# First token block of the experts stage taken through seven block products, with its first weight set prepared inside the attention

## The chip, the cores and the metric

One core of a Trainium2 chip runs the whole program. The metric is the device time of one execution in microseconds (us); the median of three runs is given, and one further execution was recorded by the hardware profiler. TensorE is PE in the rows (its weight loads PEld), VectorE DVE, ScalarE ACT, GpSimd POOL, and SP is the engine that issues DMAs.

## The reference

An attention with a bias that a small network makes from relative positions is followed by a dense layer that takes the maximum of three products:

```python
scores = scale * np.matmul(q, k.transpose(0, 1, 3, 2)) + bias   # (4, 8, 576, 576)
attn = exp(scores - max); attn /= sum(attn) + 1e-9
attn_out = np.matmul(attn, v)                                   # (4, 8, 576, 64)
x = attn_out.transpose(0, 2, 1, 3).reshape(2304, 512)
h = np.maximum(np.maximum(x @ w1, x @ w2), x @ w3)              # 2304 x 768
out = h @ w_out                                                 # 2304 x 512
```

## The kernel before, in words

**Stages.** A bias stage (0 to about 47 us of the trace) makes the bias; the attention follows (to 262 us), then the products with w1, w2, w3 (to 463 us, `moe`) and the products with w_out (to the end). Every product of the last two stages is made of three matmuls on values split into a high and a low half (`high` is a cast on ScalarE, `low` a subtraction on VectorE or GpSimd): high by high, low by high, high by low.

**The attention** runs in 72 steps (`Attention.step`, step n = 9 * pair + y, where y = 4 is a mixed step of leftovers), and four more that drain it (72 to 75). Step n makes the scores of step n (`front`, tile `s`), turns the exponentials of step n-4 on TensorE (`flip`, tiles `tp` and `lp`, one buffer each way, freed by copies `et` on ScalarE and VectorE), multiplies turned blocks by v (`pv`), then adds bias and takes the maximum on VectorE (`shift`, `sn`, `nm`), takes the exponentials on ScalarE (`expo`, tile `e`) and normalizes those of step n-2 on GpSimd (`norm`, with the reciprocal `rc` on VectorE in even steps). The order of each engine is the order of the program text; no engine overtakes itself.

**Work placed into the steps.** `step(n, more)` calls the entries of `more` at two places: `between()` stands behind the step's exponentials (in steps 18 to 71 ahead of `norm`, in the drain behind it) and moves each entry by one piece of vector or GpSimd work; at the step's end one entry moves by one piece of ScalarE work. The entries are generators that mark which kind comes next: `w0` (`first`, conversion of three weight sets of 64-bit values to 32 bits, five pieces for each half of a set), `pend` (queued pieces on GpSimd, in steps with y = 3, 5, 8), `ex` (`early_x`) and `lx` (`late_x`), which split the first token block into halves. `prep` puts casts and low halves of q and k into the steps with y = 0, 1, 3, 4.

**Token blocks and weight sets.** The attention's output lies in blocks b11, b12, b21, b22 of three token blocks x = 0, 1, 2 (`raws`, slots `r{x}_{k}`, k = 0 to 3 for b12, b11, b21, b22). A weight set s is a 512 x 256 part of one of w1, w2, w3; there are nine. Sets 1 to 8 use seven block products (`group`), for which each token block also needs the sums t1 = b12 - b11, t3 = b22 - b12, t2 = t3 + b11, t4 = b21 - t2 and each set four sums of its blocks. Set 0 is multiplied with all three token blocks in eight block products each (`plain`). One block product is six matmuls of 384 columns (`terms`). A product may add onto the PSUM bank of an earlier one (`made(p, on)`); before that the earlier value has been copied out.

**Slots.** A tile takes the slot of its tag. Where an older tile of the same tag is still in use, the first writer of the new tile waits for every reader of the old one, also for readers that stand behind it in the program text. `home` (class `Blocks`) puts the high half of t3 into r{x}_0, its low half into r{x}_1, and those of t2 into r{x}_2 and r{x}_3, the slots of raw b12, b11, b21 and b22.

**Order of the products before.** plain(0), plain(1), plain(2), then the groups of set 1. `jobs` holds, for each product slot, the casts, sums and low halves of token blocks that are emitted ahead of it.

Of the kernel before, what the change touches and what calls it, by code (L numbers as in the profile page):

```python
# [19 lines left out]
def kernel(  # L20
# [191 lines left out]
    class Attention:  # L212
# [204 lines left out]
        def step(self, n, more=()):  # L417
# [36 lines left out]
            def empty():  # L454
                tp0, tp1, left = self.flip(f)
                if lead and n < NSTEP:
                    for h in range(2):
                        self.shift(n, h)
                    if split:
                        self.expo(n, 0)  # L460
                shared = n < NS + 2
                for x in tp0 + ([] if shared else left):
                    nc.scalar.copy(*x)  # L463
                if turned:
                    products()
                for x in tp1 + (left if shared else []):
                    nc.vector.tensor_copy(*x)  # L467
# [172 lines left out]
    def moe(pool, wpool, x0, xa, xb, raw, sr):  # L640
# [15 lines left out]
        def plain(x, slot):  # L656
            for t in range(2):
                for b in range(2):
                    o = bank(f"c{b}{t}_{x}")[:, 0:TW]
                    for d in range(2):  # L660
                        n = (("b11", "b12"), ("b21", "b22"))[d][t]
                        terms(o, wf[0], xs[x][n], 256 * (2 * d + b), d == 0, d == 1)
                        if d:
                            nc.scalar.copy(ht[:, x, 2 * b + t], o)
                        slot()

        def group(s, x):
# [14 lines left out]
            def p1():  # L682
                o["m1"] = keep("m1", 2)
                nc.scalar.copy(o["m1"], made("p1"))
# [50 lines left out]
        def raise_w(s, k):  # L735
            raw, sr = made_w[s]
            if k == 0:
                p = wpool if s % 2 == 0 else pool
                wf[s] = tuple(p.tile([128, 1792], F32R, tag=f"w{c}{s % 2}", bufs=1, name=f"w{c}{s}") for c in "hl")
# [12 lines left out]
        for k, what in enumerate((  # L752
                (F(b1.high, "b11", "b21"), F(b0.sum, "t4")),
                (F(b1.low, "b11"), F(b1.high, "b12"), F(b0.high, "t2")),
                (F(b1.low, "b21"), F(b1.high, "b22")),
                (F(b1.low, "b12"),),
                (F(b1.low, "b22"), F(b2.high, "b11")),
                (F(b0.low, "t2"), F(b2.high, "b21")),
                (F(b1.sum, "t1"), F(b2.high, "b12")),
                (F(b2.low, "b11"), F(b2.high, "b22"), F(b1.high, "t1")),  # L760
                (F(b2.low, "b21"), F(b0.high, "t4")),
                (F(b2.low, "b12"),),
                (F(b2.low, "b22"),),
                (F(b0.low, "t4"),),
                (F(b1.low, "t1"),),
                (F(b1.sum, "t3"),),
                (F(b1.sum, "t2"), F(b1.high, "t3")),
                (F(b1.low, "t3"),),
                (F(b1.sum, "t4"), F(b1.high, "t2")),
                (F(b1.low, "t2"), F(b1.high, "t4")),  # L770
                (F(b1.low, "t4"), F(raise_w, 1, 0)),
                (F(b2.sum, "t1"), F(raise_w, 1, 1)),
                (F(lower_w, 1, 0, v, 3), F(b2.high, "t1")),
                (F(lower_w, 1, 3, v, 4),),
                (F(b2.low, "t1"),),
                (F(b2.sum, "t3"),),
        )):
            at(k // 8, k % 8, *what)
        at(3, 0, F(b2.sum, "t2"), F(b2.high, "t3"))
        at(3, 1, F(b2.low, "t3"))  # L780
        at(3, 3, F(b2.sum, "t4"))
        at(3, 4, F(b2.high, "t2"))
        at(3, 5, F(b2.low, "t2"))
        at(3, 6, F(b2.high, "t4"))
        at(4, 2, F(b2.low, "t4"))
# [228 lines left out]
        def out_pair(m):  # L1014
# [23 lines left out]
            def p1():  # L1038
                o["m1"] = keep("m1", 2)
# [47 lines left out]
        for x in range(NX):  # L1087
            now[:] = [x, 0]
            plain(x, slot)
# [14 lines left out]
    with tc.manual_schedule():  # L1104
# [44 lines left out]
        class Pieces:  # L1149
# [18 lines left out]
        def first():  # L1168
            todo = [(w_srcs(s, d), f"{s}_{d}") for s in (PARK, 0, 1) for d in range(2)]
# [8 lines left out]
            def sums(raw, name, k=None):  # L1178
# [12 lines left out]
                return [lambda n=n: piece(n) for n in range(4)]  # L1191

            def block(name):
                made = []

                def half(d):
                    if d == 0 and name == "2":
                        made.append(apool.tile([128, 1024], F32, name="wr2", bufs=1))
                    elif d == 0:
                        if name == "1":  # L1200
                            pend.rest()
                        made.append(raw_tile(wpool, 1))
                    return made[0][:, 512 * d:512 * d + 512].bitcast(U32)

                return made, half
# [3 lines left out]
            made, half = block("2")  # L1209
            for d in range(2):  # L1210
                yield from conv(lambda: half(d), f"2_{d}")
            nc.sync.dma_start(out=w_d[0, 0], in_=made[0])
            pend.extend(sums(made[0], "2", 0))
            hi, lo = (wpool.tile([128, 1792], F32R, tag=f"w{c}0", bufs=1, name=f"w{c}0") for c in "hl")
            wf[0] = (hi, lo)
            made, half = block("0")
            for d in range(2):
                r = slice(512 * d, 512 * d + 512)
                yield from conv(lambda: half(d), f"0_{d}")
                raw = made[0]  # L1220
                yield "scalar"
                nc.scalar.copy(hi[:, r], raw[:, r])
                pend.extend(lambda k=k, raw=raw: arith(nc.gpsimd, part(lo, k), part(raw, k), part(hi, k))
                            for k in range(2 * d, 2 * d + 2))
            made, half = block("1")
            for d in range(2):
                yield from conv(lambda: half(d), f"1_{d}")
            for f in sums(made[0], "1"):
# [7 lines left out]
        def early_x():  # L1236
            g = nc.gpsimd
            for k in ("b12", "b11"):
                yield "scalar"
                x0.high(k)  # L1240
                yield "vector"
                x0.low(k, g)
# [6 lines left out]
            x0.low("t1", g)  # L1249

        def late_x():
            for k in ("b21", "b22"):
                yield "scalar"
                x0.high(k)
                yield "vector"
                x0.low(k, nc.gpsimd)

        ex, lx = Stream(early_x()), Stream(late_x())
        while n < NSTEP + LAG:
            more = []  # L1260
            early = n // NS in (4, 5) and n % NS in (6, 7, 8)
            if n >= NS - 2 and n % NS in (0, 2, 4, 6, 7) and not (early and n != 4 * NS + 6):
                more += [w0]
            if n % NS in (3, 5, 8):
                more += [pend]
            if early:
                more.insert(0, ex)
            if n >= NSTEP:
# [7 lines left out]
        x0.sum("t3")  # L1276
        x0.high("t3")
        x0.sum("t2")
        x0.low("t3")
# [53 lines left out]
```

## Time and profile before

| | |
|---|---|
| median of three runs | 534.36 us (534.30 to 534.59) |
| the profiled execution, whole | 534.26 us |
| its span, first to last instruction | 532.4 us |
| TensorE busy (its weight loads) | 98% (82%) of the span |
| VectorE, ScalarE, GpSimd busy | 81%, 67%, 50% |
| mean granted TensorE clock | 1.00 of full speed |

Busy time of TensorE counts overlapping matmuls, whose ends are modelled, so that 98% doesn't say that it runs at its peak; the start of one matmul to the start of the next of the same kind says more. Step n's start is taken here as the start of its first score matmul.

### The profile page before, as it was taken

How to read it: one execution, taken by the hardware profiler on the slowest of the kernel's cores; microseconds unless marked ns; L12 is line 12 of the kernel's file. 1: busy time of each engine (PE TensorE's matmuls, PEld its weight loads, DVE VectorE, ACT ScalarE, POOL GpSimd, SP SyncE). 2: the span in 40 equal slices, each digit the busy share in tenths (PEclk: the TensorE clock that was granted, in tenths of full speed). 3: DMA queues.
4: the chain of work that ended last, by engine and by line, in shares of the span. 5: the costliest groups of instructions: out<-in, count | busy, mean ns of one | idle time of the engine just before them, and what ended most of it. 6: DMA issues, size and time to landing. Idle time of an engine off the chain costs nothing.

```text
span 532.4 us, 13650 instructions
## 1 busy us (share of the span) xinstructions
PE 524.1 (98%) x5191; PEld 437.6 (82%) x5191; DVE 431.9 (81%) x922; ACT 357.9 (67%) x803; POOL 265.0 (50%) x295
## 2 busy tenths in 40 slices
PE   9999899999999999999999999999999999999997
PEld 5455667676767676767799999999999999999997
DVE  7998979898988798987698988648887456898883
ACT  6998989998989998988566443443434325464552
POOL 0003878678878888776501663646565535300000
PEclk9999999999999999999999999999999999999999
DMA  5895998533865183212201215442175440856642
GB/s 151 244 336 175 319 303 227 174 106 110 239 200 151 25 240 122 67 23 48 97 0 41 79 42 197 139 159 79 57 259 180 142 145 2 252 175 188 191 146 81
DMA packets 73458, 78.66 MB, mean 148 GB/s; under 512 B 23152, under 2 KB 54512, under 8 KB 73392
## 3 DMA queue, kind: packets, MB, share of 16 engines
q1 hardware_dynamic: 73248, 77.49, 46.9%
q8 instruction: 41, 0.67, 0.5%
q10 hardware_dynamic: 144, 0.29, 0.2%
q14 instruction: 25, 0.20, 0.1%
HBM read 49.56 MB, written 27.94 MB: 146 GB/s over the span
## 4 chain that ended last, share of the span: by engine, by line
PE 94%; ACT 3%; DVE 2%; issue 1%; DVEq 0%
PE pv L393 16%; PE p L654 11%; PE p L653 11%; PE p L652 11%; PE s L287 11%; PE bp L135 7%; PE tp L352 6%; PE p_o L1029 4%; PE p_o L1030 4%; PE p_o L1028 4%; ACT e L311 2%; PE lp L352 2%; PE c L652 2%; PE c L653 2%; PE c L654 2%; PE s L277 1%
## 5 line engine op out<-in xcount | busy, mean ns | idle before, releaser
L325 POOL TENSOR_SCALAR e<-e,rc 128x576 f32<-128x576 f32 x144 | 109.5, 776 | 34.5 <-DVE rc L321 30.1
L297 DVE CUSTOM_DVE_ANT_0 sn<-s,bias 128x576 f32<-128x576 f32 x144 | 103.1, 754 | 25.2 <-PE lp L352 13.8
L311 ACT ACTIVATE e<-sn,nm 128x576 f32<-128x576 f32 x144 | 111.3, 779 | 3.7 <-DVE nm L297 3.6
L393 PE MATMUL pv<-et,vt 128*64 128x320 f32 (+1 forms) x496 | 74.0, 419 | 0.1
L467 DVE COPY et<-tp 128x512 f32<-128x512 f32 x72 | 49.3, 685 | 6.2 <-PE tp L352 6.1
L352 PE MATMUL tp<-ident,e 64*128 64x64 f32 x1152 | 53.0, 224 | 0.5 <-ACT et L463 0.3
L542 POOL TENSOR_TENSOR wl<-wr,wh 128x256 fp32r<-128x256 f32 x25 | 24.4, 999 | 58.3 <-ACT wh L740 58.3
L463 ACT COPY et<-tp 128x512 f32<-128x512 f32 x72 | 41.8, 580 | 14.8 <-PE lp L352 13.8
L287 PE MATMUL s<-kh,qh 64*128 64x288 f32 x240 | 48.0, 341 | 1.1 <-DVE nm L297 0.9
L352 PEld LDWEIGHTS tp<-ident,e 64*128 64x128 f32 x1152 | 47.3, 139 | 0.8 <-ACT et L463 0.4
L287 PEld LDWEIGHTS s<-kh,qh 64*128 64x128 f32 x240 | 28.0, 184 | 21.4 <-DVE nm L297 9.1
L393 PEld LDWEIGHTS pv<-et,vt 128*64 128x64 f32 x496 | 30.2, 136 | 17.8 <-issue 1.4
L287 PE MATMUL s<-kl,qh 64*128 64x288 f32 x240 | 40.9, 296 | 0.0
L135 PE MATMUL bp<-hid,w2s 128*32 128x79 f32 (+51 forms) x640 | 40.1, 391 | 0.4 <-DVE hid L113 0.3
L287 PE MATMUL s<-kh,ql 64*128 64x288 f32 x240 | 39.8, 290 | 0.0
L113 DVE TENSOR_SCALAR hid<-sm,bp 128x528 f32<-128x528 f32 (+17 forms) x108 | 39.1, 448 | 0.0
L692 ACT COPY u<-p 128x384 f32<-128x384 f32 x24 | 11.5, 480 | 40.7 <-PE p L654 40.6
L135 PEld LDWEIGHTS bp<-hid,w2s 128*32 128x32 f32 x640 | 20.2, 110 | 20.7 <-issue 14.4
L699 ACT COPY u<-p 128x384 f32<-128x384 f32 x24 | 11.5, 479 | 37.1 <-PE p L654 37.1
L542 POOL TENSOR_TENSOR wl<-ws,wh 128x256 fp32r<-128x256 f32 x28 | 29.1, 1068 | 13.1 <-ACT wh L742 13.1
L352 PE MATMUL lp<-ident,e 64*128 64x64 f32 x144 | 33.2, 230 | 2.0 <-ACT et L463 0.8
L542 DVE TENSOR_TENSOR q<-p,u 128x384 f32<-128x384 f32 x36 | 20.0, 554 | 16.2 <-ACT u L699 13.8
(231 smaller groups left out, 1618.3 us busy)
## 6 DMA issues: line engine op xcount, KB each, us to landing
bias_d<-bs SPq DMA_DIRECT2D x36, 295.5 KB, 4.9
bias<-bias_d SPq DMA_DIRECT2D x16, 576.0 KB, 5.4
w<-in_moe_w_dram SPq DMA_DIRECT2D x36, 256.0 KB, 3.3
h_d<-ht SPq DMA_DIRECT2D x18, 384.0 KB, 3.2
hin<-h_d SPq DMA_DIRECT2D x16, 384.0 KB, 4.5
qr<-in_qd_dram SPq DMA_DIRECT2D x16, 288.0 KB, 4.3
kr<-in_kd_dram SPq DMA_DIRECT2D x16, 288.0 KB, 4.8
vt<-in_v_dram SPq DMA_DIRECT2D x32, 128.0 KB, 3.2
```

Source lines behind the costliest of these rows:

```text
L135: nc.tensor.matmul(bp[32 * c:32 * c + 32, o:o + w], lhsT=w2s, rhs=src, start=True, stop=True)
L287: nc.tensor.matmul(ss[h][:, x, 0:HALF], lhsT=u[q][p, 128 * t:128 * t + 128], rhs=u[k][p, cols], start=(j == 0), stop=(j == len(terms) - 1))
L297: nc.vector.tensor_tensor_reduce(out=sn.rearrange("p (a b) -> p a b", a=2), in0=st["s"][h][:, :, 0:HALF], in1=bt.rearrange("p (a b) -> p a ...
L311: nc.scalar.activation(st["e"][:, S * h:S * h + S], sn, ACTF.Exp, scale=-1.0, bias=nm, accum_out=self.sm[:, x:x + 1])
L325: nc.gpsimd.tensor_scalar(out=e, in0=e, scalar1=self.rc[:, x:x + 1], scalar2=1.0, op0=ALU.mult, op1=ALU.mult)
L352: return nc.tensor.transpose(to, e2[p, k0:k0 + 128], ident[p, p])
L393: nc.tensor.matmul(pv[p], lhsT=w, rhs=x, start=(c == 0), stop=(c == NTQ))
L467: nc.vector.tensor_copy(*x)
L542: eng.tensor_tensor(out=out, in0=f(a), in1=f(b), op=op)
L652: nc.tensor.matmul(o, lhsT=hi[:, c], rhs=h[:, j], start=first and j == 0, stop=False, **on)
L653: nc.tensor.matmul(o, lhsT=hi[:, c], rhs=l[:, j], start=False, stop=False, **on)
L654: nc.tensor.matmul(o, lhsT=lo[:, c], rhs=h[:, j], start=False, stop=last and j == 1, **on)
```

## The change

- The products begin with `group(0, 0)`, seven block products of set 0 and token block 0, among which the first product of `plain(1)` stands as sixth; the rest of plain(1) and plain(2) follow: 23 products where there were 24. The slots of `jobs` are renumbered, and the sums, casts and low halves of token block 0 leave it.
- Weight set 0 is converted first, ahead of sets 2 and 1. All its eight parts get low halves on GpSimd (before, four), and its four sums are made on GpSimd, as pieces of `pend`. The high half is cast in three pieces: 768 and 256 columns at the end of a step, and the 1024 columns of the sums inside a piece of `pend`.
- `pend` moves by two pieces in steps with y = 3 and y = 8, unless `ex` is in the same step, and by one in those with y = 5.
- `early_x` loses b12's two halves; `late_x` gets the sums t3, t2, t4 and the halves of t3 and t2 and runs also in steps 69 and 70. t4's halves follow the drain.
- In the attention's steps 4 and 5 the copies of `lp` move from VectorE to ScalarE. The buffer `m1` has one copy, not two.

```diff
-                shared = n < NS + 2
+                shared = FILL + 2 <= n < NS + 2
...
-        def plain(x, slot):
-            for t in range(2):
-                for b in range(2):
-                    o = bank(f"c{b}{t}_{x}")[:, 0:TW]
-                    for d in range(2):
-                        n = (("b11", "b12"), ("b21", "b22"))[d][t]
-                        terms(o, wf[0], xs[x][n], 256 * (2 * d + b), d == 0, d == 1)
-                        if d:
-                            nc.scalar.copy(ht[:, x, 2 * b + t], o)
-                        slot()
+        def plain(x):
+            o = {}
+
+            def product(t, b, d):
+                if d == 0:
+                    o[t, b] = bank(f"c{b}{t}_{x}")[:, 0:TW]
+                n = (("b11", "b12"), ("b21", "b22"))[d][t]
+                terms(o[t, b], wf[0], xs[x][n], 256 * (7, 0, 1, 2)[2 * d + b], d == 0, d == 1)
+                if d:
+                    nc.scalar.copy(ht[:, x, 2 * b + t], o[t, b])
+
+            return [lambda t=t, b=b, d=d: product(t, b, d) for t in range(2) for b in range(2) for d in range(2)]
...
-                o["m1"] = keep("m1", 2)
+                o["m1"] = keep("m1", 1)
...
-        for x in range(NX):
-            now[:] = [x, 0]
-            plain(x, slot)
+        c1, c2 = plain(1), plain(2)
+        g0 = list(group(0, 0))
+        for k, f in enumerate(g0[:5] + c1[:1] + g0[5:] + c1[1:] + c2):
+            now[:] = (0, k) if k < 7 else divmod(k + 1, 8)
+            slot()
+            f()
...
             def go(self, scalar):
-                if self.todo and not scalar:
-                    self.todo.pop(0)()
+                if not scalar:
+                    for f in self.todo[:self.count]:
+                        self.todo.pop(0)()
...
-            todo = [(w_srcs(s, d), f"{s}_{d}") for s in (PARK, 0, 1) for d in range(2)]
+            todo = [(w_srcs(s, d), f"{s}_{d}") for s in (0, PARK, 1) for d in range(2)]
...
+            raw0 = apool.tile([128, 1024], F32, name="wr0p", bufs=1)
+            yield from whole(raw0, 0)
+            hi, lo = wf[0] = tuple(wpool.tile([128, 2048], F32R, tag=f"w{c}0", bufs=1, name=f"w{c}0") for c in "hl")
+            yield "scalar"
+            nc.scalar.copy(hi[:, 0:768], raw0[:, 256:1024])
+            nc.scalar.copy(hi[:, 1792:2048], raw0[:, 0:256])
+            make, got = sums(raw0, "0")
+
+            def low0(k):
+                if k == 3:
+                    nc.scalar.copy(hi[:, 768:1792], got["sr"])
+                src = part(raw0, (k + 1) % 8) if k in (0, 1, 2, 7) else part(got["sr"], k - 3)
+                arith(nc.gpsimd, part(lo, k), src, part(hi, k))
+
+            lows = [lambda k=k: low0(k) for k in (0, 1, 2, 7, 3, 4, 5, 6)]
+            pend.extend(lows[:4] + make + lows[4:])
...
         def early_x():
-            g = nc.gpsimd
-            for k in ("b12", "b11"):
-                yield "scalar"
-                x0.high(k)
-                yield "vector"
-                x0.low(k, g)
+            yield "scalar"
+            x0.high("b11")
+            yield "vector"
+            x0.low("b11", nc.gpsimd)
...
         def late_x():
-            for k in ("b21", "b22"):
-                yield "scalar"
-                x0.high(k)
-                yield "vector"
-                x0.low(k, nc.gpsimd)
+            yield "vector"
+            x0.sum("t3", 0)
+            yield "scalar"
+            x0.high("b21")
+            yield "vector"
+            x0.sum("t3", 1)
+            yield "scalar"
+            x0.high("t3")
+            yield "vector"
+            x0.sum("t2")
+            yield "scalar"
+            x0.high("b22")
+            yield "vector"
+            x0.low("t3")
+            x0.low("b21", nc.gpsimd)
+            yield "scalar"
+            x0.high("t2")
+            yield "vector"
+            x0.sum("t4")
+            x0.low("b22", nc.gpsimd)
+            yield "vector"
+            x0.low("t2")
...
-            early = n // NS in (4, 5) and n % NS in (6, 7, 8)
+            early = n // NS in (4, 5) and n % NS in (6, 7, 8)[:3 - n // (5 * NS)]
...
             if n % NS in (3, 5, 8):
+                pend.count = 1 if early or n % NS == 5 else 2
                 more += [pend]
             if early:
                 more.insert(0, ex)
-            if n >= NSTEP:
+            if n >= NSTEP or n in (NSTEP - 3, NSTEP - 2):
                 more.insert(0, lx)
...
         for w in (w0, pend, ex, lx):
             w.rest()
-        x0.sum("t3")
-        x0.high("t3")
-        x0.sum("t2")
-        x0.low("t3")
+        x0.high("t4")
+        x0.low("t4")
         at.split_x()
```

## Rows read from the trace of the kernel before

**Rows 1.** Windows: attention; stretch, length, busy time (count) by engine, clock, DMA.
```profile
75.00:249.00 174.00, 172.93 (x2364) 121.00 (x2362) 150.47 (x407) 160.63 (x431) 137.83 (x158) 1.00 0.47 139
```

**Rows 2.** One line's instructions: name, count, ns min/median/max, first to last start.
```profile
L652 PEld LDWEIGHTS p<-b11h,wh x48: 187/188/188, 286.9 to 453.4; 128*128 128x128 f32 x48
...
L652 PEld LDWEIGHTS c<-b11h,wh x12: 186/188/188, 262.0 to 281.2; 128*128 128x128 f32 x12
```

**Rows 3.** Timeline of VectorE, step 4: start, us, engine, line, operation, count, idle.
```profile
56.51 0.28 DVE L467 COPY et<-lp 128x128 f32<-128x128 f32 x1
```

**Rows 4.** Chain that ended last, steps 42 to 44: start, us, what.
```profile
167.45 0.72 ACT b12h L565
```

**Rows 5.** Timeline of ScalarE, step 26.
```profile
119.52 0.33 ACT L463 COPY et<-lp 128x64 f32<-128x64 f32 x2
```

**Rows 6.** Groups of instructions by line: busy us, mean ns, idle before.
```profile
L742 ACT CAST wh<-ws 128x1024 fp32r<-128x1024 f32 x8 | 8.4, 1054 | 0.0
```

**Rows 7.** Timeline of ScalarE, end of step 39.
```profile
158.97 0.65 ACT L243 CAST kh<-kr 128x576 fp32r<-128x576 f32 x1
```

**Rows 8.** Timeline of GpSimd, steps 39 to 41.
```profile
157.28 0.73 POOL L542 TENSOR_TENSOR wl<-wr,wh 128x256 fp32r<-128x256 f32 x1
157.99 1.47 POOL L325 TENSOR_SCALAR e<-e,rc 128x576 f32<-128x576 f32 x2
159.71 1.41 POOL L249 TENSOR_TENSOR kl<-kr,kh 128x576 fp32r<-128x576 f32 x1 [0.25 <-ACT kh L243]
161.62 1.47 POOL L325 TENSOR_SCALAR e<-e,rc 128x576 f32<-128x576 f32 x2 [0.50 <-DVE rc L321]
...
165.13 1.48 POOL L325 TENSOR_SCALAR e<-e,rc 128x576 f32<-128x576 f32 x2
```

**Rows 9.** Timeline of TensorE, the flip in step 43.
```profile
167.01 0.21 PE L352 MATMUL lp<-ident,e 64*128 64x64 f32 x1
```

**Rows 10.** Timelines of GpSimd and VectorE: a merge beside norms, a merge alone.
```profile
138.60 3.34 POOL L325 TENSOR_SCALAR e<-e,rc 128x576 f32<-128x576 f32 x4
...
140.28 1.05 DVE L603 SCALAR_TENSOR_TENSOR wr<-w 128x512 uint32<-128x512 uint32 x1
...
166.69 0.68 DVE L603 SCALAR_TENSOR_TENSOR wr<-w 128x512 uint32<-128x512 uint32 x1
```

**Rows 11.** Timeline of TensorE: starts of steps 44 and 46, 62 and 64.
```profile
168.78 0.46 PE L287 MATMUL s<-kh,qh 64*128 64x288 f32 x2
...
175.38 0.40 PE L287 MATMUL s<-kh,qh 64*128 64x288 f32 x2
...
221.51 0.40 PE L287 MATMUL s<-kh,qh 64*128 64x288 f32 x2
...
227.77 0.40 PE L287 MATMUL s<-kh,qh 64*128 64x288 f32 x2
```

**Rows 12.** Timeline of GpSimd, the drain.
```profile
252.62 1.47 POOL L325 TENSOR_SCALAR e<-e,rc 128x576 f32<-128x576 f32 x2 [1.02 <-DVE rc L321]
...
256.19 1.81 POOL L542 TENSOR_TENSOR b21l<-xb,b21h 128x768 fp32r<-128x768 f32 x1
```

**Rows 13.** Timeline of ScalarE, copies of the flips of steps 71 and 74.
```profile
249.49 0.58 ACT L463 COPY et<-tp 128x512 f32<-128x512 f32 x1 [0.37 <-PE tp L352]
...
256.14 0.58 ACT L463 COPY et<-tp 128x512 f32<-128x512 f32 x1 [0.45 <-PE lp L352]
256.62 0.27 ACT L463 COPY et<-lp 128x128 f32<-128x128 f32 x1
```

**Rows 14.** Timeline of TensorE, the drain: flips of steps 72, 75; first product.
```profile
250.52 0.24 PE L352 MATMUL lp<-ident,e 64*128 64x64 f32 x1 [0.43 <-ACT et L463]
...
257.94 0.27 PE L352 MATMUL lp<-ident,e 64*128 64x64 f32 x1
...
262.03 0.44 PE L652 MATMUL c<-b11h,wh 128*128 128x384 f32 x1
```

**Rows 15.** Timeline of VectorE, the drain.
```profile
260.55 0.95 DVE L542 TENSOR_TENSOR t<-xb,xb 128x768 f32<-128x768 f32 x1
```

More of the change, by code (lines that the diff above doesn't have):

```diff
@@ L738, in raise_w @@
                 p = wpool if s % 2 == 0 else pool
-                wf[s] = tuple(p.tile([128, 1792], F32R, tag=f"w{c}{s % 2}", bufs=1, name=f"w{c}{s}") for c in "hl")
+                wf[s] = tuple(p.tile([128, 1792 if s % 2 else 2048], F32R, tag=f"w{c}{s % 2}", bufs=1, name=f"w{c}{s}") for c in "hl")
                 nc.scalar.copy(wf[s][0][:, 0:768], raw[:, 256:1024])
@@ L752, in moe @@
         for k, what in enumerate((
[L753 to L756, printed above, removed]
+                (F(b1.high, "b11", "b21"), F(b1.low, "b11")),
+                (F(b1.low, "b21"), F(b1.high, "b12")),
+                (F(b1.low, "b12"), F(b1.high, "b22")),
                 (F(b1.low, "b22"), F(b2.high, "b11")),
[L758 to L761, printed above, removed]
+                (F(b1.sum, "t1"), F(b2.high, "b21")),
+                (F(b2.low, "b11"), F(b2.high, "b12")),
+                (F(b1.high, "t1"), F(b2.low, "b21"), F(b2.high, "b22")),
+                (F(b1.low, "t1"),),
                 (F(b2.low, "b12"),),
                 (F(b2.low, "b22"),),
-                (F(b0.low, "t4"),),
-                (F(b1.low, "t1"),),
                 (F(b1.sum, "t3"),),
@@ L776, in moe @@
                 (F(b2.sum, "t3"),),
-        )):
[L778 to L785, printed above, removed]
+                (F(b2.sum, "t2"), F(b2.high, "t3")),
+                (F(b2.low, "t3"),),
+        )):
+            at(*((0, k) if k < 7 else divmod(k + 1, 8)), *what)
+        at(3, 0, F(b2.sum, "t4"))
+        at(3, 1, F(b2.high, "t2"))
+        at(3, 2, F(b2.low, "t2"))
+        at(3, 3, F(b2.high, "t4"))
+        at(3, 5, F(b2.low, "t4"))
         def reload(s, k):
@@ L1038, in p1 @@
             def p1():
-                o["m1"] = keep("m1", 2)
+                o["m1"] = keep("m1", 1)
                 nc.scalar.copy(o["m1"], made("p1"))
@@ L1189, in piece @@
                     return got["sr"]
[L1191 to L1205, printed above, removed]
+                return [lambda n=n: piece(n) for n in range(4)], got
@@ L1207, in first, with whole @@
+            def whole(raw, s):
+                for d in range(2):
+                    yield from conv(raw[:, 512 * d:512 * d + 512].bitcast(U32), f"{s}_{d}")
             for _ in range(3):
                 yield "vector"
[L1209 to L1220, printed above, removed]
-                yield "scalar"
[L1222 to L1225, printed above, removed]
@@ L1226, in first @@
-            for d in range(2):
-                yield from conv(lambda: half(d), f"1_{d}")
-            for f in sums(made[0], "1"):
+            raw0 = apool.tile([128, 1024], F32, name="wr0p", bufs=1)
[4 more added lines that the diff above has]
+            nc.scalar.copy(hi[:, 1792:2048], raw0[:, 0:256])
@@ new lines, in first, with half @@
+            make, got = sums(raw0, "0")
[6 more added lines that the diff above has]
+            pend.extend(lows[:4] + make + lows[4:])
+            for s in (PARK, 1):
+                for d in range(2):
+                    if d == 0:
+                        made = []
+                    def half(s=s, d=d, made=made):
+                        if d == 0:
+                            if s == 1:
+                                pend.rest()
+                            made.append(raw_tile(wpool, 1))
+                        return made[0][:, 512 * d:512 * d + 512].bitcast(U32)
+                    yield from conv(half, f"{s}_{d}")
+                if s == PARK:
+                    nc.sync.dma_start(out=w_d[0, 0], in_=made[0])
+                    pend.extend(sums(made[0], "2", 0)[0])
@@ L1229, in first @@
+            for f in sums(made[0], "1")[0]:
                 yield "vector"
@@ L1248, in early_x @@
             yield "vector"
-            x0.low("t1", g)
+            x0.low("t1", nc.gpsimd)
         def late_x():
-            for k in ("b21", "b22"):
-                yield "scalar"
-                x0.high(k)
-                yield "vector"
-                x0.low(k, nc.gpsimd)
+            yield "vector"
[20 more added lines that the diff above has]
+            x0.low("t2")
         ex, lx = Stream(early_x()), Stream(late_x())
```

## The prediction

> **What bounds the kernel now.** I read the clock first, then busy time by engine over the attention [rows 1], then TensorE's start times of equal work, and last the timelines of the engines around each step that gets new work. In the attention TensorE is busy for 172.9 of 174.0 us at a clock of 1.00 [rows 1], but its busy time counts overlapping matmuls, and ScalarE, busy for 160.6, isn't far behind: a step there has two limits close to each other, and a short delay of either moves all that follows. In the products there is one limit: plain product after plain product starts without a gap, 24 of them from 262.0 to 286.9 us, 1.04 us each, and set 1 follows at once [rows 2]. So a product taken out there is worth its length, while what the change does in the attention is worth what it delays there. All times below are those of the profiled run (534.26 us, of which 532.4 are the span; the rest should not change); it stands 0.10 below the median.
>
> **One product less: -1.04.** 48 half products of set 0 become 42, that is 24 times 1.04 us less one [rows 2]. The first group needs t2, t3, t4 and their halves early; at the drain's 0.95 us for each sum or low half on VectorE t2's would be done near 263.5 and t4's near 265.6, and by the terms below the first product comes later than both. I take no gap.
>
> **Copies of lp in steps 4 and 5 to ScalarE: -0.20.** VectorE's copy (0.28 us) stands straight ahead of the next step's bias addition [rows 3]. Without it that starts about 0.2 earlier. Bounds: -0.25 and 0.
>
> **Casts of set 0, end of step 25: +0.40.** ScalarE then casts 768 and 256 columns, where it now takes 512 absolute values. A 768-column cast takes 0.72 [rows 4], the 256 columns a third of that; together some 0.4 us more than now. The copies of lp that stand behind them at 119.52 [rows 5] come later by that, and the flip that waits for their bank starts directly behind them. Bounds 0 and 0.5. The 512-column casts that leave steps 33 and 45 I cost at nothing (low bound -0.1).
>
> **Two pieces of set 0 in step 39: +2.35.** Here `pend` moves by two: the last sum on GpSimd and a low half. The second brings a cast of the 1024 columns of sums, 1.05 us [rows 6], and it is issued inside the vector piece, so behind step 39's exponentials, where ScalarE now starts the cast of kh at 158.97 [rows 7]. It ends at 160.02. GpSimd has done its sum at 158.0 and then stands until 160.1 for that cast, and queued behind it on GpSimd are the low half itself (0.73), the norm that now starts at 157.99, k's low half, and two more norms [rows 8]. The first norm starts at 160.8, 2.8 late. Idle time to take this up is 0.25 and 0.50 [rows 8]. The norm that now ends at 166.6 so ends near 168.65, and the flip that reads it now starts at 167.01 [rows 9]: it had 0.4 to spare, TensorE stands still for 1.65. Now VectorE's work in between: a clamp in step 40 and the merge in step 42, which now runs in a gap of GpSimd (at 166.69). Beside norms such a merge takes 1.05 us and four half norms 3.34; alone the merge takes 0.68 [rows 10], the half norms 2.94 (twice the 1.47 of [rows 8]). So they get in each other's way, by 0.4 us each time on GpSimd. Bounds for each of the two are 0 and 0.68; I take 0.5 each, a little over the 0.4, since GpSimd is late after the change and has no gap left: 1.05 in all with what rounds up. Against that `early_x` is lighter: b12's cast (0.72, on the chain that ended last [rows 4]) is gone; steps 44 and 45 take 6.60 us where steps 62 and 63 of the same kinds take 6.26 [rows 11], so up to 0.35 comes back. 1.65 + 1.05 - 0.35 = 2.35. Low bound 1.35, with nothing for VectorE; high bound 2.7.
>
> Where two pieces stand in other steps (26, 30, 35, 48, 53), GpSimd's next norm waits for a reciprocal anyway, as by 0.50 in [rows 8] and by 1.02 in [rows 12]; that hides the second piece and I cost it at nothing. If the cover were gone each would cost its 0.73. The write of set 2, now issued by SP in steps 42 and 53, has nothing behind it that anyone awaits. One m1 buffer costs nothing: the addition that reads it is done before the next copy into it.
>
> **The drain, casts of b21 and t3 at the ends of steps 69 and 70: +0.4.** Two casts of 0.72 each [rows 4] stand ahead of a copy of the flip in step 71, at 249.49 with 0.37 of idle before it [rows 13], and the flip of step 72 waits for that copy already, 0.43 long [rows 14]. Of the 1.44 I take 0.8 as what reaches that copy, since the two steps have some idle of ScalarE too, and less the 0.37 that is 0.4. Bounds 0 and 1.07.
>
> **The drain, the high half of t2: +4.1.** This is the largest term, and it is a wait. The cast t2h is issued on ScalarE in step 73 and goes into the slot of raw b21, so it waits for all readers of raw b21: the low half b21l on GpSimd (step 73) and the sum t4 on VectorE, which stands behind t2h in the text (step 74). Queued behind t2h on ScalarE are the copies of the flip of step 74, now at 256.14 and 256.62 [rows 13]; they free the banks for the flip of step 75, at 257.94 now [rows 14], and behind that stand the last pv products and the first product of the next stage at 262.03. In the kernel before those copies have only 0.45 us of idle ahead of them.
>
> When are the readers done? Before, GpSimd runs norms from 252.62 and 254.76 and b21l from 256.19 for 1.81 [rows 12], VectorE takes 0.95 for a sum of two blocks [rows 15]. After, ScalarE's 0.8 lets the first norm start at 253.2. If the two engines ran freely beside each other, GpSimd would end b21l at 253.2 + 1.47 + 1.47 + 1.81 = 258.0, with gaps 258.2, and VectorE t4 at 258.25. t2h would run 258.35 to 259.07, the two copies would take 0.75, and the flip of step 75 would start at 259.95: 2.0 late, of which 0.4 is in the term above, so 1.6. If they exclude each other while VectorE has two inputs there, it is a sum: from 253.15, t2 0.95, norm 1.47, t3l 0.95, norm 1.47, t4 0.95, b21l 1.81 end at 260.75, and the same tail gives 262.45 for the flip: 4.5 late, 4.1 of it here. Rows of before show both engines longer by some 0.4 us where they meet [rows 10], of 0.68 of overlapped work; that is nearer to exclusion than to none, and I take 4.1, with 1.6 as the low bound. The excess over 4.1 I bound at 1.0, one more b21l half in the way.
>
> The Trainium skill states the rule behind this, in "SBUF — State Buffer", section "Who interferes with whom": a VectorE instruction with two inputs in SBUF and a GpSimd instruction that reads SBUF share a pair of ports, and whichever holds it blocks the other for its whole length. By that rule the drain gives +4.5, without it +2.0. The trace agrees in direction, 1.05 against 0.68 us and 3.34 against 2.94 [rows 10], though the sum of what was lost there, 0.77, is shared by the two.
>
> **Sum.** -1.04 - 0.20 + 0.40 + 2.35 + 0.4 + 4.1 = +6.0: 534.26 + 6.0 = 540.3 us.
>
> **Rivals.** *The engines don't exclude each other.* Then step 39 costs 1.35 and the drain 2.0: -1.04 - 0.20 + 0.40 + 1.35 + 2.0 = +2.5, 536.8 (535.9 to 538). For it: only part of the overlap was lost in [rows 10]. Against it: those rows all the same.
>
> *TensorE has room that its rows don't show.* Its matmul ends are modelled, so it may stand ready at the flips of steps 41 to 43 and 75 well before the rows say, or the last flips may be awaited by other things; then the waits of step 39 and of t2h fall into that room. It decides from 2.7 us of hidden room in step 43 and 4.1 in step 75 on. The time is 534.26 - 1.04 - 0.20 + 0.40 = 533.4, faster than before by 0.84. Against it: ScalarE's copies in the drain are released by TensorE with 0.37 and 0.45 idle [rows 13], so both wait on one another closely, and room of that size would be seen there.
>
> *TensorE's clock falls in the drain.* A stand of over 4 us ahead of the flip of step 75 doesn't occur in the attention before, whose clock is 1.00 all through [rows 1]. If it fell to the lower of its two levels there, 1.2 of 2.4 GHz, the last pv products, from 258.6 to 262.0 us (3.4 us at the full clock), would take twice that: 543.7. "TensorE: Matmul & The Clock Gate" of the Trainium skill, section "What's actually happening", states that the lower level is what an idle TensorE goes back to; no row of before shows it here.
>
> *The product saved is given back.* If the halves of t2 or t4 are late for the first group, TensorE waits there, up to the 1.04 that was saved: 541.3. It takes a drain in which VectorE is late by as much as TensorE is.
>
> **How the numbers follow.** Forecast 540.3: 0.45 (its own range 538.5 to 541.5, from the bounds of the two large terms). No exclusion, 536.8: 0.25. Hidden room, 533.4: 0.20 (532.9 to 534.8, with the small terms at either bound and some of the waits left). Clock, 543.7: 0.06. Product given back: 0.04. The range for 8 in 10 leaves out the clock case and 0.14 of the hidden-room case: 534.0 to 542.2. Faster by over 0.2% (1.07 us, about what a measurement of this kernel can tell from no change) means under 533.3, a little under half of the hidden-room case: 0.09. Within 0.2%: the rest of it, and 0.02 for the second case below its bound, 0.13. Slower: 0.78.
>
> **What would show it.** The products: 23 of 1.04 us between the first product and set 1's first. Step 39: GpSimd idle for about 2 us ahead of a low half, released by ScalarE's cast wh, then 2 us of idle on TensorE spread over the flips of steps 41 to 43; starts of later steps are later by that, and by no more up to step 68. The drain: ScalarE idle ahead of t2h, released by GpSimd's b21l or VectorE's t4, and TensorE idle ahead of the flip of step 75; the stage's first product at 266 to 267 where it was at 262.03. If b21l is as long as the 1.81 of before and the norms beside t2 and t3l as short as 1.47, exclusion was wrong. If the flip of step 75 starts on time, the reading of the slot was wrong, and the time falls to the low end or below.

## The result, and the profile after

The changed kernel takes 539.97 us (median of four runs, 538.46 to 540.28) against 534.48 of the kernel before on the same chip: a ratio of 1.0102, interval 1.0089 to 1.0115. The prediction was 540.3. It was right in its sign, its size and its two main mechanisms, but the sum came out as well as it did partly because misses of both signs met in it. The profiled run has a span of 538.5 us, 6.1 more than before.

Where did the 6.1 go? The table follows the shift of equal events, start in the changed kernel less start before, along TensorE's program: first score matmuls of steps, flips, first and last products, last matmul of all.

| place | shift reached, us | change there | forecast |
|---|---|---|---|
| step 4 | 0.02 | | |
| step 7 on (lp copies of steps 4, 5) | -0.09 | -0.11 | -0.20 |
| step 28 (casts of step 25) | 0.34 | +0.44 | +0.40 |
| step 39 | 0.26 | -0.08 | 0 |
| step 47 (two pieces in step 39) | 2.12 | +1.86 | +2.35 |
| step 64 (steps 60 to 62) | 2.53 | +0.41 | 0 |
| flip of step 74 (casts of steps 69, 70) | 2.84 | +0.31 | +0.4 |
| flip of step 75 (t2h's wait) | 6.16 | +3.32 | +4.1 |
| first product (clock) | 7.85 | +1.69 | 0 (a rival) |
| end of the products | 6.83 | -1.02 | -1.04 |
| last matmul | 6.06 | -0.77 | 0 |

The busy time by engine over the same 174 us of the attention, as in [rows 1], shows the loss only as a little less work of every engine but GpSimd:

```profile
75.00:249.00 174.00, 171.06 (x2326) 118.80 (x2324) 149.14 (x402) 158.76 (x423) 141.22 (x163) 1.00 0.48 139
```

TensorE's busy time fell from 172.9 to 171.1 us and the columns say no more than that. The timelines do. GpSimd in steps 39 to 41 (start, duration, operation; in brackets the idle time ahead and its releaser), to be held against [rows 8]:

```profile
157.54 0.75 POOL L542 TENSOR_TENSOR ws<-wr0p,ws 128x256 f32<-128x256 f32 x1
160.34 0.73 POOL L542 TENSOR_TENSOR wl<-ws,wh 128x256 fp32r<-128x256 f32 x1 [2.06 <-ACT wh L1212]
161.06 1.63 POOL L325 TENSOR_SCALAR e<-e,rc 128x576 f32<-128x576 f32 x2
162.66 1.42 POOL L249 TENSOR_TENSOR kl<-kr,kh 128x576 fp32r<-128x576 f32 x1
164.04 1.48 POOL L325 TENSOR_SCALAR e<-e,rc 128x576 f32<-128x576 f32 x2
```

GpSimd stands for 2.06 us between the two pieces of the step, until ScalarE's cast wh lands, and the norm that began at 157.99 begins at 161.06. The gaps that stood ahead of the next two operations (0.25 and 0.50) are used up. ScalarE's side of it, and the two flips on TensorE that wait for norms (before, no flip of these steps waited for GpSimd):

```profile
159.24 1.03 ACT L1212 CAST wh<-ws 128x1024 fp32r<-128x1024 f32 x1
160.17 0.67 ACT L243 CAST kh<-kr 128x576 fp32r<-128x576 f32 x1
```

```profile
162.74 0.27 PE L352 MATMUL lp<-ident,e 64*128 64x64 f32 x1 [0.46 <-POOL e L325]
...
169.52 0.27 PE L352 MATMUL lp<-ident,e 64*128 64x64 f32 x1 [1.16 <-POOL e L325]
```

0.46 and 1.16 are 1.6 of the 1.86 us. The drain, GpSimd, VectorE, ScalarE and TensorE in turn, beside [rows 12 to 15]:

```profile
255.83 4.15 POOL L325 TENSOR_SCALAR e<-e,rc 128x576 f32<-128x576 f32 x4 [1.23 <-DVE rc L321]
259.94 2.49 POOL L542 TENSOR_TENSOR b21l<-xb,b21h 128x768 fp32r<-128x768 f32 x1
262.40 1.80 POOL L542 TENSOR_TENSOR b22l<-xb,b22h 128x768 fp32r<-128x768 f32 x1
```

```profile
255.58 0.93 DVE L542 TENSOR_TENSOR t<-t,xb 128x768 f32<-128x768 f32 x1
...
257.60 1.04 DVE L542 TENSOR_TENSOR t3l<-t,t3h 128x768 fp32r<-128x768 f32 x1
...
259.69 1.08 DVE L542 TENSOR_TENSOR t<-xb,t 128x768 f32<-128x768 f32 x1
```

```profile
257.53 0.27 ACT L463 COPY et<-lp 128x128 f32<-128x128 f32 x1
262.47 0.83 ACT L565 CAST t2h<-t 128x768 fp32r<-128x768 f32 x1 [4.67 <-POOL b21l L542]
263.21 0.58 ACT L463 COPY et<-tp 128x512 f32<-128x512 f32 x1
263.69 0.27 ACT L463 COPY et<-lp 128x128 f32<-128x128 f32 x1
```

```profile
253.77 0.24 PE L352 MATMUL lp<-ident,e 64*128 64x64 f32 x1 [1.15 <-ACT et L463]
...
264.10 0.24 PE L352 MATMUL lp<-ident,e 64*128 64x64 f32 x1 [2.99 <-ACT et L463]
...
269.88 0.44 PE L652 MATMUL p<-b11h,wh 128*128 128x384 f32 x1
```

ScalarE has nothing to do from 257.8 to 262.47: t2h waits for the end of b21l (259.94 + 2.49), and the two copies of the flip stand behind it. TensorE idles 2.99 us ahead of the flip of step 75, and that flip's row names ScalarE's copy. From the flip to the first product it then takes 5.78 us, where it took 4.09. That is the clock: in the windows after the flip (the number ahead of the last two is the granted clock)

```profile
264.00:270.00 6.00, 5.90 (x47) 3.47 (x48) 3.04 (x7) 2.95 (x5) 0.20 (x1) 0.72 0.01 4
```

0.72 is granted, a mixture of the full and the half level, against 1.00 everywhere around the drain before.

### The profile page after: what moved, and what is told of

Its sections match the earlier page's. It is cut to its first block, busy times and chain, and to the rows that moved or that the text cites. A ratio compares the mean times of both kernels' runs of the same rounds, so it can differ in the third digit from the quotient of the medians.

```text
span 538.5 us, 13673 instructions
## 1 busy us (share of the span) xinstructions
PE 523.9 (97%) x5185; PEld 435.4 (81%) x5185; DVE 433.3 (80%) x924; ACT 358.9 (67%) x805; POOL 271.6 (50%) x302
## 4 chain that ended last, share of the span: by engine, by line
PE 50%; POOL 1%; ACT 0%; DVE 0%; issue 0%
PE p L652 11%; PE p L654 11%; PE p L653 11%; PE p_o L1029 4%; PE p_o L1028 4%; PE p_o L1027 4%; PE c L652 1%; PE c L654 1%; PE c L653 1%; PE pvlast L393 1%; POOL b21l L542 0%; POOL e L325 0%; PE pv L393 0%; ACT t2h L565 0%; ACT et L463 0%; PE tp L352 0%
## 5 line engine op out<-in xcount | busy, mean ns | idle before, releaser
L325 POOL TENSOR_SCALAR e<-e,rc 128x576 f32<-128x576 f32 x144 | 111.6, 792 | 29.2 <-DVE rc L321 25.9
L542 POOL TENSOR_TENSOR wl<-wr,wh 128x256 fp32r<-128x256 f32 x21 | 21.3, 1041 | 60.0 <-ACT wh L742 60.0
L542 POOL TENSOR_TENSOR wl<-ws,wh 128x256 fp32r<-128x256 f32 x32 | 32.1, 1028 | 15.1 <-ACT wh L744 13.0
L352 PEld LDWEIGHTS lp<-ident,e 64*128 64x128 f32 x144 | 19.7, 137 | 20.8 <-issue 11.8
```

Of the source, the lines that this page charges most:

```text
L325: nc.gpsimd.tensor_scalar(out=e, in0=e, scalar1=self.rc[:, x:x + 1], scalar2=1.0, op0=ALU.mult, op1=ALU.mult)
L352: return nc.tensor.transpose(to, e2[p, k0:k0 + 128], ident[p, p])
L542: eng.tensor_tensor(out=out, in0=f(a), in1=f(b), op=op)
```

## Experiments

**The slot alone.** t2h goes into a slot that nothing else uses at that time, and t4h, which is made behind the drain, into the one that t2h had. No instruction moves.

```diff
         def home(self, n, k):
+            if self.x == 0 and k == 0 and n in ("t2", "t4"):
+                tag = dict(t2="f0_0", t4="r0_2")[n]
+                return self.xa.tile(SHAPE, F32R, tag=tag, bufs=1, name=f"{n}h_0")
```

> The changed kernel with one edit: the slots of the high halves of t2 and t4 are exchanged, so t2h no longer goes into the slot of raw b21. Order and work stay. Theory (the cast waits for the readers of raw b21, and the copies of the flip wait behind it): ScalarE's 4.67 us of idle ahead of t2h are gone, TensorE's 2.99 ahead of the flip of step 75 fall below 0.5, and the clock stays at 1.00 in the drain, so the 1.7 us that the last products lost there come back as well: about 535.0 where the changed kernel took 540.0. Rival (the flip waits because norms and low halves on GpSimd are late, whatever the slot): 539.5 to 540. Second rival (the lower clock has nothing to do with the wait): the wait goes, the clock stays low, 537.

Measured: 535.92 us (535.30 to 536.23), 1.0028 of the kernel before (1.0016 to 1.0039); 4.05 less than the changed kernel by the medians. ScalarE, then TensorE:

```profile
257.35 0.27 ACT L463 COPY et<-lp 128x128 f32<-128x128 f32 x1
257.51 0.85 ACT L568 CAST t2h<-t 128x768 fp32r<-128x768 f32 x1
258.80 0.59 ACT L463 COPY et<-tp 128x512 f32<-128x512 f32 x1 [0.45 <-PE lp L352]
```

```profile
260.87 0.27 PE L352 MATMUL lp<-ident,e 64*128 64x64 f32 x1
...
264.95 0.44 PE L655 MATMUL p<-b11h,wh 128*128 128x384 f32 x1
```

t2h starts behind the copy without a gap, the flip of step 75 starts 3.2 us earlier with no idle time of its own, and the clock is 1.00 all through. b21l is as long as it was (2.52), and so are the four half norms (4.15): that GpSimd is late doesn't matter once ScalarE doesn't wait for it. The rival is refuted: the price came through the slot. The first product is at 264.95, a shift of 2.92, of which 2.35 were there at the last step of the attention; the drain costs 0.57 without this wait. The forecast of 535.0 was 0.9 too low: it took the changed kernel's own time as the base, which held a shorter last stage (-0.77) that this run didn't have.

**The cast of step 39.** The sums are made first, and their 1024 columns are cast in two halves by ScalarE at the ends of steps 29 and 38; each step keeps its number of GpSimd pieces.

```diff
-                if k == 3:
-                    nc.scalar.copy(hi[:, 768:1792], got["sr"])
...
-            pend.extend(lows[:4] + make + lows[4:])
+            pend.extend(make + lows)
+
+            def cast(k):
+                nc.scalar.copy(hi[:, 768 + 512 * k:1280 + 512 * k], got["sr"][:, 512 * k:512 * k + 512])
...
-                    yield from conv(half, f"{s}_{d}")
+                    yield from conv(half, f"{s}_{d}", (2 + d, lambda d=d: cast(d)) if s == PARK else None)
```

> The changed kernel with set 0's sums ahead of its low halves, and the cast of their 1024 columns made as two casts of 512 at the ends of steps 29 and 38, where ScalarE waits for TensorE. Number of pieces per step stays. Theory (GpSimd's wait of 2.06 us for that cast in step 39 and what is queued behind it): the 1.85 us that steps 39 to 46 lose are gone, all but 0.3: 538.2 to 538.5. Rival (it is two pieces in one step, or VectorE's merge beside the norms): at most 0.7 come back, 539.3 or more. Second rival (the two casts cost as much where they are now): 540.

Measured: 539.08 us (537.47 to 540.13), above the forecast of 538.2 to 538.5. GpSimd in step 39:

```profile
157.42 0.74 POOL L542 TENSOR_TENSOR wl<-wr0p,wh 128x256 fp32r<-128x256 f32 x1
158.12 0.74 POOL L542 TENSOR_TENSOR wl<-ws,wh 128x256 fp32r<-128x256 f32 x1
158.83 1.48 POOL L325 TENSOR_SCALAR e<-e,rc 128x576 f32<-128x576 f32 x2
```

Two pieces stand in the step as in the changed kernel, and no wait between them. From step 39 to step 47 the shift falls from 0.14 to -0.08 us: all of the 1.86 is back, and 0.2 more, which fits the lighter `early_x` (not tested apart). So it was the wait for the cast, not two pieces in a step, and the casts cost nothing at ends of steps where ScalarE waits for TensorE anyway (0.34 us of idle time are left behind the second one). The time is less telling than the trace here. The first product starts 2.3 us earlier than in the changed kernel (267.58 for 269.88), but the last stage, 0.77 shorter than before in that kernel's profiled run, is 0.24 longer than before in this one. The drain is still there, with 4.67 us of wait on ScalarE, and the clock's part of it varies (below). The 0.41 us of step 60 are still there too.

**Do VectorE and GpSimd exclude each other?** This kernel leaves out the low half of t3 of token block 0; its high half is multiplied in its place. That takes 1.04 us from VectorE beside the last two norms and nothing from GpSimd.

```diff
-            x0.low("t3")
+            x0.out["t3"] = (x0.hi["t3"], x0.hi["t3"])
```

> The changed kernel without the low half of t3 of token block 0 (its high half is multiplied in its place): VectorE does 1.04 us less beside the last two norms. GpSimd's own work is the same. Theory (VectorE with two inputs and GpSimd exclude each other): the four half norms from 255.8 take 0.6 to 0.9 us less than their 4.15, b21l ends that much earlier, and so do t2h and the flip of step 75; 539.2 to 539.4. Rival (no exclusion, GpSimd's work is long for another reason): these norms stay at 4.15, the flip moves by less than 0.1, 540.

Measured: 538.51 us in a single execution (span 536.7, clock 1.00), 1.8 us below the profiled run of the changed kernel. Most of that is the clock: the flip of step 75 to the first product takes 4.09 us here, for 5.78. GpSimd, VectorE and ScalarE:

```profile
256.02 3.45 POOL L325 TENSOR_SCALAR e<-e,rc 128x576 f32<-128x576 f32 x4 [1.23 <-DVE rc L321]
259.44 1.81 POOL L542 TENSOR_TENSOR b21l<-xb,b21h 128x768 fp32r<-128x768 f32 x1
```

```profile
259.73 2.33 DVE L542 TENSOR_TENSOR t<-xb,t 128x768 f32<-128x768 f32 x1
```

```profile
262.15 0.83 ACT L565 CAST t2h<-t 128x768 fp32r<-128x768 f32 x1 [4.16 <-DVE t L542]
```

The four half norms take 3.45 where they took 4.15, though their own work is the same: exclusion, as the theory had it. The surprise is behind them. Now b21l starts first, at 259.44, and takes its lone 1.81; t4's sum starts 0.29 later and takes 2.33 where it takes 0.95 alone ([rows 15]). It ends 0.8 us behind b21l's end, as if it had done almost nothing while b21l ran. Here whoever is first keeps the other out, and t2h, which needs both, waits for the sum of the two: its releaser is now VectorE's sum. So the 0.70 gained on the norms brought the flip of step 75 only 0.5 us: it starts at 263.77 here and at 264.10 in the changed kernel, and less the shifts that stood at step 71 (2.72 and 2.53) that is 261.05 against 261.57. The Trainium skill says in "SBUF — State Buffer", "Who interferes with whom", that the ports which the two engines share are an exclusive lock, and that the order of issue decides who blocks. The trace agrees: 2.33 against 0.95.

**All waits taken out, first attempt.** Here the three losses are removed together: sums first; casts at the ends of steps 29 (768 columns), 38 (256 and 512) and 43 (512), none in step 25; b21h and b22h in steps 72 and 73 as before the change; t3h and t2h at the end of step 74, t2h in its own slot; t3l in step 75 and t4's sum behind the drain.

> The changed kernel with its waits taken out: sums of set 0 first; its casts at the ends of steps 29 (768 columns), 38 (256 and 512) and 43 (512) instead of 25 and 39; casts of b21 and b22 at the ends of steps 72 and 73 as before; t2h and t3h at the end of step 74, t2h in a slot of its own; t4's sum behind the drain. Theory (the losses are these waits and nothing else): the drain is as long as before the change, steps 25 to 46 lose at most 0.3, one product less is left: 533.0, faster than before by 1.2 to 1.5. Rival (VectorE's and ScalarE's added work itself is on the path): 534.5 to 536.

Measured: 538.37 us (537.15 to 539.54), worse than forecast by 5. The profiled execution, 537.15 at a clock of 1.00, is 4.1 above the forecast, for two reasons that are this edit's own; three of the five executions have a lower mean clock (0.997) and took 1.2 to 2.4 us more than it. In the attention the shift is -0.15 at step 46 and 2.36 at step 54. VectorE in step 49:

```profile
186.74 0.69 DVE L467 COPY et<-tp 128x512 f32<-128x512 f32 x1
189.79 1.23 DVE L606 SCALAR_TENSOR_TENSOR wr<-w 128x512 uint32<-128x512 uint32 x1 [2.37 <-POOL ws L542]
```

Without a ScalarE piece in step 25 the conversion runs one of its steps ahead, and its merge for set 1 forces out what is left in `pend`: three sums in one step on GpSimd, with VectorE, and behind it the next bias addition, waiting 2.37 us for them. In the drain nothing is lost (shift 2.34 at step 71 and at the first product), but the third product waits:

```profile
265.16 0.84 ACT L568 CAST t4h<-t 128x768 fp32r<-128x768 f32 x1 [3.32 <-DVE t L542]
265.90 0.82 ACT L568 CAST b11h<-xb 128x768 fp32r<-128x768 f32 x1
266.63 0.82 ACT L568 CAST b21h<-xb 128x768 fp32r<-128x768 f32 x1
267.36 0.47 ACT L689 COPY m<-p 128x384 f32<-128x384 f32 x1
```

```profile
267.89 0.44 PE L655 MATMUL p<-t2h,wh 128*128 128x384 f32 x1 [1.17 <-ACT m L689]
```

The copy that must be made before that product may add onto its bank stands behind three casts, the first of which waits for t4's late sum. TensorE starts it 1.51 us behind the matmul ahead of it, where 0.17 is usual. This is the rival "the product saved is given back", made by this edit.

**Second attempt.** The conversion keeps its steps (a cast of 256 columns stays in step 25), and set 1's second half runs one step later, so that steps 60 and 61 hold the vector work that they held before the change. t3l and t4 are made in the drain ahead of the copies of step 75.

```diff
-                for token in convert(wpool, ahead.pop(0), out, name):
+                for k, token in enumerate(convert(wpool, ahead.pop(0), out, name)):
+                    if cast and k == cast[0]:
+                        yield "scalar"
+                        cast[1]()
+                    if name == "1_1" and k == 1:
+                        yield "vector"
                     yield token
...
+            yield "scalar"
+            x0.high("t3")
+            x0.low("t3")
+            x0.high("t2")
+            yield "vector"
+            x0.sum("t4")
```

> The version before this one lost 2.5 us in steps 47 to 54 and 1.5 ahead of the third product, by its own edits: its conversion ran one step early, so all sums of set 2 were emitted at once ahead of VectorE's merge in step 49, and the copy that frees the third product's bank stood behind three casts that waited for t4. Here: casts of set 0 at the ends of steps 25 (256 columns), 29 (768), 38 and 43 (512 each), the conversion's steps as in the changed kernel but set 1's second half one step later from step 60 on, and t3l and t4 in the drain ahead of the copies of step 75. Theory (the change loses by waits alone): steps 25 to 46 no longer than before the change, the 0.4 us of steps 60 to 62 gone as well, drain as long as before, one product less: 533.1 to 533.4, faster by 0.9 to 1.3. Rival (added work is on the path somewhere): 534.3 or more.

Measured: 533.66 us (533.27 to 534.09, eleven runs) against 534.42: 0.9984 of the kernel before, interval 0.9975 to 0.9993, a little above the forecast. It beats both kernels, the one before by 0.8 us. The shift is -0.27 at step 7, has no jump at step 28 or at step 62, and is -0.53 at step 71. So the 0.44 of the casts in step 25 and the 0.41 of step 60 were these pieces in those steps. The drain still costs 0.44 (first product at -0.09), and the rows of VectorE and TensorE show what it pays now:

```profile
257.13 1.75 DVE L542 TENSOR_TENSOR t3l<-t,t3h 128x768 fp32r<-128x768 f32 x1 [0.88 <-ACT t3h L568]
258.80 0.68 DVE L467 COPY et<-tp 128x512 f32<-128x512 f32 x1
259.40 1.97 DVE L542 TENSOR_TENSOR t<-xb,t 128x768 f32<-128x768 f32 x1
```

```profile
259.63 1.95 PE L393 MATMUL pvlast<-et,vt 128*64 128x256 f32 x16 [0.21 <-DVE et L467]
```

Beside b21l and b22l each takes about double its 0.95: t3l ends 0.81 us behind b21l's end (258.07), t4's sum 0.82 behind b22l's (260.55). The copy of step 75 stands behind t3l, and the last pv products wait for it: they start at 259.63, where 259.77 less the 0.52 of before the drain would be 259.25. The products bring -0.74 instead of -1.02.

**The changed kernel, twice more.** What of its 6.1 us is the kernel's, and what the single execution's?

> The changed kernel once more, unchanged. Theory (its wait in the drain lets the clock fall in some executions, by more or less, and the last stage's shorter distance between matmuls, 113.3 for 117.8 ns from about 505 us on, belongs to that execution and not to the change): the waits of 2.06 and 4.67 us stand to 0.05 as before, while the time lost after the flip of step 75 may be anything from 0 to 1.7 us, and the last stage may keep 117.8. Rival (both belong to the changed program): 1.7 lost and 0.77 gained again.

> As the run before it, for a second look: the waits the same; if the clock loss or the last stage's gain differs between the looks, it is the execution's.

Measured: spans of 539.3 and 537.5 us. ScalarE's wait is 4.68 in both, TensorE's 3.00 in both, GpSimd's 2.06 in both. But the flip of step 75 to the first product takes 5.74 us in the first, at a granted clock of 0.72, and 4.09, as before the change, in the second:

```profile
264.00:270.00 6.00, 5.94 (x57) 4.46 (x58) 4.68 (x9) 3.45 (x7) 0.16 (x1) 1.00 0.01 4
```

```profile
264.06 0.24 PE L352 MATMUL lp<-ident,e 64*128 64x64 f32 x1 [3.00 <-ACT et L463]
...
268.15 0.44 PE L652 MATMUL p<-b11h,wh 128*128 128x384 f32 x1
```

Equal waits, different clocks: the loss of about 1.7 is the execution's. The wait makes it likelier, but isn't needed for it. A mean clock of 0.997 or less, as in the profiled executions with the fall, stands in 7 of 10 executions of the kernels in which TensorE stands 3.0 us ahead of that flip (the changed one and the cast experiment). It also stands in 3 of 5 of the first attempt, in whose profiled execution no stand is over 1.72 us, and in 2 of the 28 of the kernel before that have a clock on record (535.51 and 535.58 us, about 1.1 over its median), but in none of the 18 of the slot experiment and the second attempt (no stand over 1.2 us in the profiled ones). Where the clock fell in those of the first attempt and of the kernel before no trace shows.

And the last stage keeps 117.8 ns from matmul to matmul in both, up to 525 us at least, so the -0.77 of the profiled run (113.3 from about 505 us on) isn't the change either.

## Why the prediction was right, point by point

**What bounds the kernel.** Borne out: the products took 1.02 less for the one left out (forecast 1.04), starting back to back in both kernels ([rows 2]), and all else was decided by delays in the attention and its drain. (The prediction's "48 half products become 42" should read 46, for 24 products and 23; its term is one product, as it should be.)

**lp copies, steps 4 and 5.** Forecast -0.20, measured -0.11; only half of what I took from VectorE's row reached TensorE.

**Casts of step 25.** Forecast +0.40, measured +0.44, and gone when 768 of the columns are moved elsewhere.

**Step 39.** Forecast +2.35, measured +1.86, and the whole of it came back in the kernel that moved the cast. The wait of 2.06 was forecast as 160.1 less 158.0. What was over-sized is the term for VectorE's clamp and merge beside GpSimd (1.0): the norms stretched by 0.16 at 161.06 and by 0.4 at the merge, some 0.55 in all. (The low bound written there as 1.35 is 1.30 by its own terms, 1.65 less 0.35.)

**Steps counted at nothing.** One stretch wasn't: +0.41 in steps 60 to 62. I listed what each piece costs on GpSimd and ScalarE, and let the vector pieces that only move by a step go at nothing. VectorE's bias addition in step 60, before and after:

```profile
217.46 0.76 DVE L297 CUSTOM_DVE_ANT_0 sn<-s,bias 128x576 f32<-128x576 f32 x1 [0.23 <-PE lp L352]
```

```profile
219.93 0.76 DVE L297 CUSTOM_DVE_ANT_0 sn<-s,bias 128x576 f32<-128x576 f32 x1 [0.58 <-ACT e L311]
```

Less the shift of 2.12 it starts 0.35 later, behind ScalarE's exponentials, and the scores of step 61 stand behind it. The last kernel gave it back by moving the pieces (0.23 of wait there, as before). Why the addition waits for ScalarE with the pieces one step earlier stays open.

**The drain, casts of steps 69 and 70.** Forecast +0.4; 1.15 of idle ahead of the flip of step 72 where 0.43 stood, of which 0.31 is left at the flip of step 74.

**t2h's wait.** The mechanism was right in each of its links (slot, both readers, copies behind, flip, first product) and the slot experiment shows that it alone carries the price. The size was off: 3.32 by the shifts, 3.05 by what the slot gave back, for 4.1. I had taken full exclusion, all six operations one behind the other: 7.60 us from the start of t2's sum to the end of b21l. It was 6.85 (255.58 to 262.43), and these 0.75 are the miss. GpSimd's four half norms and b21l together were longer by 1.24 + 0.69 = 1.9 us than alone (2.91 and 1.80), and VectorE's three operations overlapped GpSimd's work for 2.8 of their 3.05 us: about 0.7 of the overlap was lost, and not all of it. [rows 10] would have given something near it (0.40 for 0.68), had I used the row's own ratio and not gone to the end that it was nearest to.

**The clock.** Held at 0.06 and as an alternative to the forecast; it came on top of it, in two of three profiled executions of the changed kernel and in that of the cast experiment, where TensorE stood 2.99 to 3.00 us; it stayed away in the third with the same 3.00, and in the kernel without t3l, where TensorE stood 2.74 us. My error was to set the case apart from the forecast: with the wait it came in 7 of 10 executions, so it belonged to it, as +1.7 in part of them, though the runs above show that it isn't bound to this wait. The price was 1.7 and not 3.4, as only part of the pv products ran at the lower level: sixteen of the last twenty took 3.01 us (from 266.50) where they took 1.90 before, the four behind them 0.60 as before. The Trainium skill, "TensorE: Matmul & The Clock Gate", "What's actually happening", says of the rise at a kernel's start that its point differs between runs of one kernel; what differed here is whether a fall came at all.

**How the sum came out.** In the last execution above, without clock loss and without the short last stage, the change costs 537.5 - 532.4 = 5.1 us, against a forecast of 6.0. Of the four runs of the result the one without a lower clock took 538.46, 4.0 above the kernel before (its last stage isn't on record). The median holds the clock's loss, as three of the four runs do, and that filled the gap: the signs and the large terms were reasoned, but that 540.0 came out so near to 540.3 is in part luck. The rivals: exclusion does exist (against "they don't exclude each other"), no hidden room was found at any of the flips named, and the product saved was not given back in the changed kernel.

## What to carry to other kernels

A tile that takes over the slot of another waits for all readers of the old one, also those that come later in the text: for each cast or copy that is moved forward, list the readers of the slot that it will write into, and then what stands behind it on its own engine. Moving a piece of work to where its engine idles cost nothing here; putting it inside another engine's piece made that engine wait for the first one's whole queue. And where VectorE read two inputs from SBUF beside GpSimd's work, 0.7 to 0.9 of the overlapped time was lost; of two single operations the one that started second paid nearly all of it.

## What the runs showed of the hardware

TensorE's granted clock can fall after a stand of 3.0 us, and whether it does differs between executions with the same waits: 0.72 over 6 us in two executions, 1.00 in the third; it cost 1.69 and 1.65 us here. A VectorE sum with two inputs in SBUF took 0.95 us alone, 1.08 when it started 0.25 ahead of a GpSimd operation (which then took 2.49 for 1.80), and 2.33 when it started 0.29 behind one of 1.81. In the last stage equal matmuls follow each other at 117.8 ns up to 500 us in all nine traces; two change to 113.3 at about 505 us, five only after 520 and two not at all, at a granted clock of 1.00 in all; what decides that isn't settled.
